# An attention and feed-forward kernel: nine tokens to a partition, head groups on partition halves, x made transposed by wide matmuls

## Chip, cores, metric

One core of one Trainium2 chip. The metric is device time in microseconds (us) of one execution, lower is better; most executions of one kernel agree within 1% (the kernel before: 299.02 to 300.62 in the four beside the changed kernel). Bandwidths are for this one core. "PE" is TensorE's matmul side, DVE VectorE, ACT ScalarE, POOL GpSimd, SP SyncE, which issues nearly all the DMAs.

## The reference, cut to what matters

```python
# q, k, v: (8 batches, 8 heads, 576 tokens, 64) float32
q_s = softmax(q, axis=-1)            # over the 64 of a head
k_s = softmax(k, axis=2)             # over the 576 tokens
kv  = einsum('bhsd,bhse->bhde', k_s, v)
x   = einsum('bhsd,bhde->bhse', q_s, kv)   # -> (8, 576, 512) after the transpose of heads
xn  = (x - mean(x)) / sqrt(var(x) + 1e-6) * g_ln
out = x + relu(xn @ w_ch1) @ w_ch2   # 512 -> 2048 -> 512, all float32
```

## The kernel before: the parts that matter

The feed-forward runs on blocks of 512 tokens (four to a partition, "main"); the last 64 tokens of each batch ("remainder") are collected into a ninth block. `mm1` is the first product (64 matmuls of 512 columns), `mm2_split` the second, done with seven products instead of eight on quarter blocks. A small scheduler in Python orders the instructions; each engine then runs its own list in order (ACT of the changed kernel: a cast of v waits 4.06 us for its load until 110.25, and three relus of matmuls that ended by 108.2 start only after it, from 111.32). Names in the code and the profiles: `stg` are the buffers in which loads land, `ek` and `eq` the exponentials of k and q, `eqT` is `eq` transposed, `vb` is v cast to 16 bits, `kve` (changed kernel) is k'v divided by the softmax sum, `xsT` is x transposed, `ot` the output before its store.

```python
def load_main(b, src):                       # q, k or v: 4 heads at a time, all 128 partitions
    for half in range(2):
        s = nxt("stg", NST)
        load(stg[s].rearrange("p (h r) -> p h r", h=4),
             src[b, 4*half : 4*half + 4, :Q0].rearrange("h (p t) d -> p h (t d)", t=J), ...)  # 1024-byte rows
def load_rem(b, src, row): ...               # the last 64 tokens: 64 partitions, 256-byte rows
# k'v, each head pair g: 4 matmuls over 128 tokens and one over 64
for t in range(KT):
    n = P if t < J else 64
    nc.tensor.matmul(pa[a][:, c0 : c0+130], ek[u][:n, t, g*P : g*P+P],
                     vb[u][:n, t, 2*g : 2*g+2, :], start=(t == 0), stop=(t == KT-1))
# x by tokens: 4 x 4 matmuls of 130 columns (the 65th of each head is the softmax sum), then
# norm(): x = numerator / sum on DVE; then x is DMA-transposed (xsT) for mm1
# ... (cut)
```

The softmax here doesn't subtract the row's maximum and nothing guards it: scores larger than these inputs give would overflow.

## Time and profile before

| | before |
|---|---|
| median of 3 runs | 299.33 us (299.02 to 300.62) |
| PE busy | 283.7 of 299.0 us |
| k'v for one batch, 20 matmuls | 1.87 us |
| undisturbed mm1, mm2 of one block | 13.81 us, 12.25 us |
| 1024-byte load packets, mean / median | 54 / 46 ns |

The last row comes from the trace's records of single DMA packets. A packet of these loads is one row (24,576 packets of 1024 bytes for 48 loads of 512 KB), moved by one of 16 DMA engines; 16 x bytes / time is the rate when all are busy. "Granted clock" (PEclk) is the profile's figure for the share of TensorE's full clock that was granted, 0.997 in the mean here.

Page of the kernel before: the span, PE's busy time, then the span in 40 slices, busy tenths of PE, granted clock, busy tenths of the DMA engines, and GB/s.

```profile
span 299.0 us, 5130 instructions
...
PE 283.7 (95%) x1992; PEld 180.7 (60%) x1992; DVE 200.9 (67%) x482; ACT 151.4 (51%) x271; POOL 22.0 (7%) x40
...
PE   8987999998899999999999999999999999999990
...
PEclk9999999999999999999999999999999999999998
DMA  6999999799799949999999990304303030030006
GB/s 198 288 386 387 367 259 270 220 160 295 239 234 233 321 90 273 343 222 206 304 269 274 244 243 20 140 0 72 140 2 70 3 140 0 2 140 1 2 0 140
```

PE is full; the DMA engines are nearly full too in most of the first 24 slices. The windows of the same kernel cut the span at the first mm1 matmul (24.18), at the first split mm2 (78.59) and at the last matmul. Columns: window, length, then busy time of PE, PEld (weight loads), DVE, ACT and POOL with instruction counts, granted clock, DMA share and GB/s.

```profile
0.00:24.18 24.18, 21.05 (x114) 9.47 (x115) 12.59 (x29) 13.71 (x20) 9.62 (x26) 1.00 0.95 298
24.18:78.59 54.41, 50.37 (x314) 27.34 (x315) 47.13 (x98) 33.62 (x57) 9.09 (x9) 1.00 1.02 281
78.59:291.60 213.01, 212.04 (x1565) 143.86 (x1564) 140.33 (x355) 104.09 (x196) 3.33 (x5) 1.00 0.56 142
291.60:299.00 7.40, 0.27 (x3) 0.00 (x0) 0.88 (x2) 0.00 (x0) 0.00 (x0) 0.87 0.64 142
...
5.00:10.00 5.00, 5.00 (x20) 2.12 (x19) 1.76 (x4) 3.17 (x3) 0.23 (x1) 1.00 1.09 316
```

In the third stretch PE idles 0.97 of 213 us (length minus PE busy), in the second 4.04. The chain of waits (start, length, what) shows one cause of the latter, a late load of v:

```profile
67.12 7.88 DMA stg<-in_v_dram
75.00 0.02 issue
75.02 0.71 DVE vb L343
75.73 0.04 issue
75.77 1.04 PE pa L364 x10
```

### The profile page before, as it was taken

The page shows a single profiled execution, that of the slowest core. Times are in us where ns is not written, and L with a number is a line of the kernel's source. Part 1 is how long each engine was busy: PE and PEld are TensorE (multiplying, and loading weights), DVE is VectorE, ACT ScalarE, POOL GpSimd, SP SyncE. Part 2 cuts the span into 40 slices and gives each one's busy share as a digit, 9 for nine tenths or more (in the row PEclk, how much of TensorE's full clock was granted, in tenths as well). Part 3 has the DMA queues.
Part 4 walks back from the last instruction along what each step waited for, and adds up shares of the span by engine and source line. Part 5 has one row for each costly group of instructions (what it writes and reads, how often), then busy time and mean ns, then how long its engine had stood idle before and what let it go on. Part 6 is the DMA issues. An engine that isn't in the chain of part 4 may idle for free.

```text
span 299.0 us, 5130 instructions
## 1 busy us (share of the span) xinstructions
PE 283.7 (95%) x1992; PEld 180.7 (60%) x1992; DVE 200.9 (67%) x482; ACT 151.4 (51%) x271; POOL 22.0 (7%) x40
## 2 busy tenths in 40 slices
PE   8987999998899999999999999999999999999990
PEld 3444445553696468645875489448747844864780
DVE  0679999995887776677786787657356436635641
ACT  3656476696443990497667740792252055025200
POOL 3432041300000000000000010000000000000000
PEclk9999999999999999999999999999999999999998
DMA  6999999799799949999999990304303030030006
GB/s 198 288 386 387 367 259 270 220 160 295 239 234 233 321 90 273 343 222 206 304 269 274 244 243 20 140 0 72 140 2 70 3 140 0 2 140 1 2 0 140
DMA packets 75127, 53.80 MB, mean 180 GB/s; under 512 B 43872, under 2 KB 68448, under 8 KB 75104
## 3 DMA queue, kind: packets, MB, share of 16 engines
q1 hardware_dynamic: 74528, 53.49, 67.1%
q8 instruction: 15, 0.25, 0.3%
q10 hardware_dynamic: 576, 0.00, 0.1%
q14 instruction: 8, 0.07, 0.1%
HBM read 36.70 MB, written 9.44 MB: 154 GB/s over the span
## 4 chain that ended last, share of the span: by engine, by line
PE 77%; DMA 9%; DVE 7%; ACT 3%; SPq 1%; issue 1%; DVEq 0%
PE pg L516 35%; PE pg L593 30%; DMA stg<-in_v_dram 8%; PE pa L364 4%; PE pg L642 4%; DMA stg<-in_q_dram 2%; PE pa L429 2%; ACT hT L481 1%; PE pg L503 1%; DVE ot L652 1%; SPq L260 1%; DVE bst L723 1%; DVE T L547 1%; DVE vb L343 1%; PE pg L316 1%
## 5 line engine op out<-in xcount | busy, mean ns | idle before, releaser
L516 PE MATMUL pg<-xsT,w_sb 128*128 128x512 f16 x544 | 120.9, 379 | 0.0
L481 ACT ACTIVATE hT<-pg 128x512 f16<-128x512 f32 x122 | 71.4, 595 | 78.9 <-PE pg L516 49.2
L516 PEld LDWEIGHTS <-w_sb 128*128 128x128 f16 x544 | 52.3, 98 | 60.4 <-DVE w_sb L319 0.3
L593 PEld LDWEIGHTS <-S 128*128 128x128 f16 x512 | 49.4, 98 | 5.9
L530 DVE TENSOR_TENSOR S<-hT 128x512 f16<-128x512 f16 x64 | 27.1, 424 | 30.0 <-ACT hT L481 29.0
L593 PE MATMUL pg<-T,S 128*128 128x256 f16 x384 | 44.4, 273 | 0.0
L593 PEld LDWEIGHTS <-hT 128*128 128x128 f16 x384 | 37.2, 98 | 6.7 <-issue 1.2
L593 PE MATMUL pg<-w_sb,hT 128*128 128x256 f16 x256 | 29.6, 272 | 0.3
L601 DVE SCALAR_TENSOR_TENSOR ot<-pg,st,cp 128x256 f32<-128x256 f32 x48 | 21.0, 479 | 12.4 <-PE pg L593 12.3
L601 DVE SCALAR_TENSOR_TENSOR cp<-pg,st,x 128x256 f32<-128x256 f32 x48 | 21.0, 478 | 10.7 <-PE pg L593 10.5
L460 ACT ACTIVATE sq<-x,st 128x512 f16<-128x512 f16 x28 | 20.2, 720 | 5.4 <-DVE st L456 5.0
L390 ACT ACTIVATE eq<-stg 128x1024 bf16<-128x1024 f32 x12 | 12.6, 1058 | 15.8 <-DMA stg<-in_q_dram 15.8
L417 DVE SCALAR_TENSOR_TENSOR x<-pa,rq 128x512 f16<-128x512 f32 x28 | 19.2, 690 | 0.8
L364 PE MATMUL pa<-vb,ek 128*128 128x130 f16 (+1 forms) x160 | 16.5, 223 | 2.9 <-DVE vb L343 2.9
L483 DVE TENSOR_SCALAR hT<-pg 128x512 f16<-128x512 f32 x22 | 15.1, 688 | 6.0 <-PE pg L516 5.6
L337 ACT ACTIVATE ek<-stg 128x1024 bf16<-128x1024 f32 x16 | 16.6, 1052 | 2.6 <-DMA stg<-in_k_dram 2.6
L364 PEld LDWEIGHTS <-ek 128*128 128x128 bf16 (+1 forms) x160 | 11.1, 97 | 9.5 <-issue 3.0
L661 PE MATMUL pg<-zero 128*128 128x512 f16 x54 | 15.5, 443 | 1.2 <-DVE zero L240 1.2
L593 PE MATMUL pg<-w_sb,S 128*128 128x256 f16 x128 | 15.6, 273 | 0.0
L593 PE MATMUL pg<-T,hT 128*128 128x256 f16 x128 | 15.5, 273 | 0.0
L530 DVE TENSOR_TENSOR S<-hT,S 128x512 f16<-128x512 f16 x32 | 14.6, 455 | 0.9
L642 PE MATMUL pg<-w_sb,hT 128*128 128x512 f16 x64 | 15.1, 379 | 0.0
(77 smaller groups left out, 217.9 us busy)
## 6 DMA issues: line engine op xcount, KB each, us to landing
stg<-in_q_dram SPq DMA_DIRECT2D x16, 512.0 KB, 7.4
stg<-in_k_dram SPq DMA_DIRECT2D x16, 512.0 KB, 8.3
stg<-in_v_dram SPq DMA_DIRECT2D x16, 512.0 KB, 6.3
stg<-in_moe_w_ch_dram SPq DMA_DIRECT2D x16, 512.0 KB, 9.4
out_dram<-ot SPq DMA_DIRECT2D x16, 512.0 KB, 2.9
rem<-in_k_dram SPq DMA_DIRECT2D x8, 128.0 KB, 7.7
rem<-in_v_dram SPq DMA_DIRECT2D x8, 128.0 KB, 3.9
rem<-in_q_dram SPq DMA_DIRECT2D x8, 128.0 KB, 5.5
```

The source lines that it names most:

```text
L337: nc.scalar.activation(ek[u][:, :J].rearrange("p t (h d) -> p h t d", h=H)[:, 4 * half : 4 * half + 4], stg[ld["k"][half]].rearrange("p (h ...
L364: nc.tensor.matmul(pa[a][:, c0 : c0 + 130], ek[u][:n, t, g * P : g * P + P], vb[u][:n, t, 2 * g : 2 * g + 2, :], start=(t == 0), stop=(t = ...
L417: plan.add("DVE", 0.76, lambda: nc.vector.scalar_tensor_tensor(dst[:, j, :].rearrange("p (h d) -> p h d", h=H), in0=pz[:, :, :D], scalar=1 ...
L460: plan.add("ACT", act_t(512, 0.15), lambda j=j: nc.scalar.activation(sq, x[:, j, :], AF.Square, bias=sti[:, 1, j : j + 1], accum_out=sti[: ...
L481: nc.scalar.activation(hT[:, m, :], pg[gi], AF.Relu)
L483: nc.vector.tensor_scalar_max(hT[:, m, :], in0=pg[gi], scalar1=0.0)
L516: nc.tensor.matmul(pg[gi], w1_sb[:, ko, m * P : m * P + P], xt[:, ko], start=(ko == 0), stop=(ko == KO1 - 1))
L530: plan.add("DVE", dve_t(512, 2), lambda: nc.vector.tensor_tensor(S[i][:, ks], a, b, op=op), r=r, w=[("S", i, k0), ("S", i, k0 + 1)])
L593: nc.tensor.matmul(pg[gi][:, 256 * i : 256 * i + 256], fa(k, i), fb(k), start=(first and i == 0 and k == 0), stop=(last and k == HK - 1), ...
L601: nc.vector.scalar_tensor_tensor(dst[:, i, :], in0=pg[gi][:, 256 * i : 256 * i + 256], scalar=sti[:, 4, 2 * t0 + i : 2 * t0 + i + 1], in1= ...
L642: nc.tensor.matmul(pg[gis[j]], hT[:, kk, j * P : j * P + P], w2_sb[:, kk, :], start=(kk == 0), stop=(kk == KO2 - 1))
L661: nc.tensor.matmul(bank_, zero[:, :P], zero, start=start, stop=start, skip_group_check=True)
```

## The change

The intent: give each partition nine consecutive tokens (576 = 64 x 9), so that a head fills 64 partitions, the remainder loads vanish, and rows grow to 9 x 64 x 4 = 2304 bytes. Heads 0 to 3 lie on partitions 0 to 63, heads 4 to 7 on 64 to 127. k'v runs on 64 rows of the array, for both halves in turn. The softmax of q is divided out before the product, so x comes out of four 512-column matmuls already transposed, as mm1 wants it, and a DMA transpose brings it back to token order for the norm's statistics and mm2. Relu moves to ACT (138 of its 144 instructions, 122 before), as do the v casts of the later batches. The core of the diff:

```diff
-    def load_main(b, src): ...   def load_rem(b, src, row): ...
+    def load_half(b, src, hf):
+        s = nxt("stg", NST)
+        for e in range(2):
+            load(stg[s][R * e : R * e + R].rearrange("p (h r) -> p h r", h=2),
+                 src[b].rearrange("(e h) (p j) d -> e p h (j d)", e=2, j=JT)[e, :, 2 * hf : 2 * hf + 2],
+                 [("stg", s, e)], 128, 0.295)
 # k'v
-                    for t in range(KT):
-                        n = P if t < J else 64
-                        nc.tensor.matmul(pa[a][:, c0 : c0 + 130], ek[u][:n, t, g * P : g * P + P], ...)
+                for j in range(JT):
+                    for e in range(2):
+                        r0 = R * e
+                        nc.tensor.matmul(pa[ab[e]][:, :130], ek[u][r0 : r0 + R, hf, j, :],
+                                         vb[u][r0 : r0 + R, hf, j].rearrange("p s d -> p (s d)"),
+                                         start=(j == 0), stop=(j == JT - 1))
 # x, transposed (kve: k'v divided by the sum, off-diagonal blocks masked to zero)
+        for g in (0, 2, 1, 3):
+            nc.tensor.matmul(pa[a], kve[u][:, g, :], et[:, g % 2, 0:8, c0 : c0 + R], start=True, stop=True)
+    def tokens(c, cls=1):
+        nc.sync.dma_start_transpose(x..., xsT...)        # then bn_stats, bn_aggr on DVE
 # stores: one of 128 partitions -> two of 64
+        for e in range(2):
+            nc.sync.dma_start(out[c].rearrange("(p j) c -> p j c", j=JT)[:, 4*hf + e : 4*hf + e + 3 : 2, :], ot[o][R*e : R*e + R])
 # ... (norm, remainder block, square sums cut)
```

## The prediction

> **What bounds the kernel now.** TensorE. The page gives PE 283.7 of 299.0 us busy, PEclk full. By windows: 0 to 24.2 us is loading and attention of batch 0; from the first mm1 matmul (24.18) to the last matmul (291.6) PE idles only about 5 us; the end takes 7.4. In the middle mm1 costs 13.81 a batch and the split mm2 12.25 (chain of waits, from 201 on); the change leaves these alone. It can touch the 24.2, about 23 us of attention matmuls (groups L364, L429 and smaller), the 5 us and the tail. DMA is saturated until 80 us (share 0.95 to 1.05); its late v load costs 2.1 us at 73.7 (chain: stg<-in_v_dram, L343, L364).
>
> **Removed, added, moved.**
> - DMA: 1024-byte rows (54 ns a packet) and 256-byte remainder rows (12,288 packets) become 2304-byte rows; 2048-byte weight rows took 88 ns, so 370 GB/s against about 320. Transposes grow from 28.7k to 32.3k rows of about 22 ns. Estimate: 25 us less DMA time, mostly off the path.
> - PE, k'v: 20 matmuls, 1.87 us a batch, become 36 on 64 rows. In the raw order of L364 a switch between 128 and 64 rows costs 100 ns (starts 152 to 160 ns apart against 55): 8 a batch, then 4. [...] the trace shows it for column halves only: L439's pairs start 14 ns apart, each 61 ns. Estimate 18 x 30 + 200 = 0.74 us a group, 1.5 a batch; without overlap 2.4.
> - PE, x: 16 matmuls of 130 columns (0.94) plus 0.37 per two batches become 4 of 512 (0.86) and 4 of 64 (0.22). Even.
> - DVE: norm (0.69+0.20+0.08, x28) and relu go; reduce (1.34 each), bn_stats (0.665), kve come. Roughly even.
> - ACT: squares go (20 us); all relu (0.595), v casts (1.2), xT copies come: about 170 us, still under PE.
> - x reaches mm1 without a DMA transpose; the transposed x is for mm2 only.
> - Last stores: 2 DMAs a half instead of 4, 0.6 us of SP issue each.
>
> **On the path.** Start: v lands again about 15.5, but kve, copies and weight centring follow faster on DVE: mm1 at about 21.4 (-2.8). DVE still limits centring (PE waits 3 us before the fifth m) and batch 1's attention, so mm1 of batch 1 starts near 59, like now. The v stall and its neighbours in 70 to 80 go: -3.5. Attention on PE: -3 over batches 1 to 7. Tail: -1.3. New stalls of in-order ACT (v cast waiting for DMA ahead of relu) and kve on DVE: +1.
>
> Sum: 299.3 - 3.5 - 3 - 1.3 + 1 = about 292. Range 287.5 to 297.5. Faster by over 2% (under 293.3): 0.58; within 2%: 0.38; slower: 0.04.
>
> **What would show it.** k'v matmuls in pairs 10 to 15 ns apart, 0.7 to 0.8 us a group of 18; first mm1 at 20.5 to 22.5; no PE gap over 1 us from 60 to 90; mm1 13.81 and mm2 12.25 unchanged; last matmul to end about 6 us; DMA share below 0.8 after 90.
>
> **What would make it wrong.** Row halves not overlapping (+6); SP blocked behind an x transpose waiting for xsT, so inputs come late (+1 to 4); ACT at 75% in mm1 holding pg banks; POOL's multiply (2.3 us, from 1.04 for 512 columns) delaying the eqT transpose and the v load gated on it.

## The result, and the profile after

312.27 us (median of 4 runs, 311.5 to 314.11) against 299.5 (4 runs): the ratio is 1.043, 95% interval 1.037 to 1.0489. It got slower. A ratio here is the mean time of one kernel's fast runs over the mean of the other's fast runs of the same rounds, so it is not quite the ratio of the medians quoted. All runs discussed are fast; slow ones, among them one run of the kernel before at 1032 us, are left out of the ratios. The changed kernel's mean granted clock was 0.984: two stretches of 3.4 us, from 23.3 and from 112.0, had a granted clock of 0.50, and both came just after gaps of PE (1.73 and 3.32 us); after the gap of 1.73 before 60.04 there was none (1.00 from 60 to 90). At half the clock they cost at most 3.4 us together (an estimate, half of twice 3.4 us). I take them for a consequence of the waiting below and not a cause of its own; no run here shows it.

The same lines of the page, after:

```profile
span 309.6 us, 5175 instructions
...
PE 280.9 (91%) x2017; PEld 173.5 (56%) x2017; DVE 197.4 (64%) x407; ACT 161.8 (52%) x258; POOL 36.6 (12%) x32
...
PE   8749798779999959999898979999999999999992
...
PEclk9997999999999979999999999999999999999998
DMA  7999999999996999269989990999993440013004
GB/s 160 267 273 386 280 332 238 236 255 214 228 226 108 196 259 217 54 159 228 233 160 234 286 181 4 210 215 224 160 269 82 83 115 22 2 23 115 0 1 138
```

PE has less to do than before (280.9 against 283.7), yet the span is 10.6 us longer: waiting, not work. The windows, cut at the same events (first mm1 27.07, first split mm2 82.60, last matmul 303.40), and two stretches in which only q, k and v load:

```profile
0.00:27.07 27.07, 19.94 (x117) 8.67 (x118) 13.43 (x27) 11.27 (x16) 3.73 (x15) 0.94 0.96 255
27.07:82.60 55.53, 47.85 (x293) 24.83 (x292) 49.62 (x86) 33.25 (x54) 11.39 (x7) 1.00 1.07 265
82.60:303.40 220.80, 212.98 (x1609) 140.03 (x1607) 133.49 (x294) 117.29 (x189) 21.44 (x10) 0.99 0.66 145
303.40:309.60 6.20, 0.09 (x1) 0.00 (x0) 0.88 (x2) 0.00 (x0) 0.00 (x0) 0.76 0.60 169
...
5.00:10.00 5.00, 4.00 (x16) 1.52 (x14) 2.42 (x3) 2.08 (x2) 0.23 (x1) 1.00 1.06 225
...
45.00:65.00 20.00, 16.17 (x116) 7.90 (x114) 17.46 (x32) 8.00 (x11) 3.42 (x3) 1.00 1.05 235
```

Read the last two lines first: the DMA engines are fully busy (1.05), and move 225 to 235 GB/s. Before, 1024-byte rows moved at 316 in the same first stretch. The rows are longer, the rate is lower. (Had half of the 16 engines stood idle, the share would be about 0.5; so all of them work, and slowly. From 45 to 65 the kernel before moved only 220 GB/s, but with 256-byte rows, transposes and stores among its packets; the first stretch is the clean comparison.) PE's timeline (start, length, line, operation; in brackets the idle time before it and who ended it) shows what that does:

```profile
20.55 0.70 PE L379 MATMUL pa<-vb,ek 64*128 64x130 f16 x18 [2.33 <-DVE vb L369]
22.97 0.94 PE L379 MATMUL pa<-vb,ek 64*128 64x130 f16 x18 [1.73 <-DVE vb L369]
...
27.07 3.22 PE L473 MATMUL pg<-xsT,w_sb 128*128 128x256 f16 x28
...
60.04 0.70 PE L379 MATMUL pa<-vb,ek 64*128 64x130 f16 x18 [1.73 <-DVE vb L369]
...
85.32 0.70 PE L379 MATMUL pa<-vb,ek 64*128 64x130 f16 x18
...
111.47 0.72 PE L379 MATMUL pa<-vb,ek 64*128 64x130 f16 x18 [3.32 <-ACT vb L372]
```

k'v itself is as cheap as hoped: the raw starts show a pair every 59 ns, its two matmuls 3 to 4 ns apart in ten of the 16 groups and 18 to 19 in six (medians of a group), and 0.63 us from a group's start to the next instruction (0.70 with the modelled end). But it waits for v: the DVE casts of v began at 19.7 and 22.2 us, where before they began at 15.4. DVE's timeline of the changed kernel shows that they had waited for the loads:

```profile
19.73 0.77 DVE L369 CAST vb<-stg 128x1152 f16<-128x1152 f32 x1 [2.17 <-DMA stg<-in_v_dram]
22.16 0.76 DVE L369 CAST vb<-stg 128x1152 f16<-128x1152 f32 x1 [1.67 <-DMA stg<-in_v_dram]
```

The packet records say it most directly:

| kernel | load packet | mean, median ns | 16 x bytes / mean |
|---|---|---|---|
| before | 1024 B | 54.0, 46 | 304 GB/s |
| changed | 2304 B | 159.9, 166 | 231 GB/s |
| before and changed: weights, in stretches of weights alone | 2048 B | 88 | 372 GB/s |

In proportion to the 88 ns of a 2048-byte weight row, a 2304-byte row would take 99 ns (an estimate). It took 160. What differs from weight rows: the load covers 64 partitions and not 128 (theory A: a load into one half of the partitions is slow); the row is 2304 bytes long (rival B); there are twice as many loads, 0.6 to 0.7 us of SP issue each (2.63 us for four loads of k at 4.87; rival C).

### The profile page after: what moved, and what is told of

Same layout as the page of the kernel before. It is cut to its first block, busy times and chain, and to the rows that moved or that the text cites. A ratio compares the mean times of both kernels' runs of the same rounds, so it can differ in the third digit from the quotient of the medians.

```text
span 309.6 us, 5175 instructions
## 1 busy us (share of the span) xinstructions
PE 280.9 (91%) x2017; PEld 173.5 (56%) x2017; DVE 197.4 (64%) x407; ACT 161.8 (52%) x258; POOL 36.6 (12%) x32
## 5 line engine op out<-in xcount | busy, mean ns | idle before, releaser
L450 ACT ACTIVATE hT<-pg 128x512 f16<-128x512 f32 x138 | 80.7, 598 | 61.5 <-PE pg L486 55.3
L486 PE MATMUL pg<-xsT,w_sb 128*128 128x512 f16 x480 | 109.3, 382 | 2.3 <-DVE ot L570 1.2
L502 DVE TENSOR_TENSOR S<-hT 128x1024 f16<-128x1024 f16 x32 | 23.8, 748 | 55.6 <-ACT hT L450 55.6
L332 POOL TENSOR_TENSOR eq<-eq,rzq 128x1152 bf16<-128x1152 bf16 x12 | 25.8, 2155 | 145.8 <-issue 52.3
L324 ACT ACTIVATE eq<-stg 128x1152 bf16<-128x1152 f32 x16 | 18.6, 1169 | 21.3 <-DMA stg<-in_q_dram 21.3
L439 DVE BATCH_NORM_STATS2 bst<-x 128x6 f32<-128x512 f16 x36 | 24.0, 668 | 5.4 <-DMA x<-xsT 5.4
L327 DVE TENSOR_REDUCE zq<-eq 128x18 f32<-128x1152 bf16 x16 | 21.4, 1340 | 7.3 <-ACT eq L324 7.3
L364 ACT ACTIVATE ek<-stg 128x1152 bf16<-128x1152 f32 x16 | 18.7, 1167 | 13.8 <-DMA stg<-in_k_dram 13.7
L379 PE MATMUL pa<-vb,ek 64*128 64x130 f16 x288 | 11.4, 220 | 10.6 <-DVE vb L369 6.6
L372 ACT CAST vb<-stg 128x1152 f16<-128x1152 f32 x12 | 14.0, 1168 | 8.1 <-DMA stg<-in_v_dram 8.0
```

The costliest lines, as they stand in the source:

```text
L324: plan.add("ACT", act_t(QW), lambda hf=hf, e=e: nc.scalar.activation(e.rearrange("p j (s d) -> p s j d", s=2), sv(lq[hf]), AF.Exp), r=sk(l ...
L327: plan.add("DVE", dve_t(QW), lambda hf=hf, eh=eh: nc.vector.reduce_sum(zq[:, hf], eh, axis=AX.X), r=[("eq", u, hf)], w=[("zq", hf)], cls=cls)
L332: plan.add(eng, dve_t(QW) if early else 2.6, lambda hf=hf, eh=eh, e2=e2: e2.tensor_tensor(eh, eh, rzq[:, hf].to_broadcast([P, 2 * JT, D]), ...
L364: plan.add("ACT", act_t(QW), lambda hf=hf: nc.scalar.activation(ek[u][:, hf].rearrange("p j (s d) -> p s j d", s=2), sv(lk[hf]), AF.Exp), ...
L379: nc.tensor.matmul(pa[ab[e]][:, :130], ek[u][r0 : r0 + R, hf, j, :], vb[u][r0 : r0 + R, hf, j].rearrange("p s d -> p (s d)"), start=(j == ...
L439: plan.add("DVE", dve_t(512), lambda j=j: nc.vector.bn_stats(bst[:, j, :], x[:, j, :]), r=[(xk, j)], w=[("bst", j)], cls=cls)
```

## The experiments

Each q/k/v experiment (e1 to e5, e7, e10) keeps the order of the compute instructions of PE, DVE, ACT and (but in e5, where POOL itself issues loads) POOL exactly as in the kernel it starts from, so that only the DMAs differ.

### e1: one load of 128 partitions

```diff
-        for e in range(2):
-            load(stg[s][64*e : 64*e+64]..., 64 partitions, 2 rows of 2304 bytes)
+        rows = src[b].rearrange("h (p j) d -> (h p) (j d)", j=JT).rearrange("(h p) r -> p h r", p=P)
+        load(stg[s].rearrange("p (h r) -> p h r", h=2), rows[:, 2*hf : 2*hf + 2], ...)
```

> The changed kernel, every engine's order kept, but each pair of 64-partition loads is one load of 128 partitions with the same 2304-byte rows (heads land at other partitions, so the result is wrong on purpose). Theory A [...]: the 2304-byte packets fall from a median of 166 ns to about 96 to 104, the first mm1 comes at 21 to 23 us instead of 27.1, and the time falls to 291 to 297 us. Theory B (rows of 2304 bytes are slow in themselves): packets stay near 165 ns and the time near 312. Theory C (twice as many DMAs, 0.6 us of issue each): packets stay as they are but the waits between them go, and the time falls.

Measured: 296.95 us against 300.87 (ratio 0.988, interval 0.9803 to 0.9957; three rounds). Its output is wrong, which doesn't matter for the time. The packets: mean 104.8, median 93 ns, 352 GB/s. The windows of e1, cut at its own first mm1, first split mm2 and last matmul:

```profile
0.00:21.79 21.79, 18.25 (x118) 8.18 (x119) 13.06 (x26) 11.22 (x16) 4.08 (x15) 1.00 0.89 326
21.79:72.78 50.99, 47.60 (x294) 24.73 (x293) 49.00 (x87) 32.72 (x55) 11.07 (x7) 1.00 0.95 280
72.78:287.20 214.42, 210.46 (x1607) 139.33 (x1607) 133.41 (x294) 115.56 (x189) 21.43 (x10) 1.00 0.55 151
287.20:293.60 6.40, 0.29 (x3) 0.01 (x1) 0.88 (x2) 0.00 (x0) 0.00 (x0) 0.89 0.57 164
...
5.00:10.00 5.00, 3.74 (x19) 1.58 (x18) 3.24 (x4) 3.06 (x3) 0.59 (x1) 1.00 1.02 379
```

The same bytes in the same rows now move at 379 GB/s in the first stretch of loads, mm1 starts at 21.79 instead of 27.07, and the profiled span falls by 16.0 us. Against the kernel before this is a gain of only 1.2%. B falls: 2304-byte rows are fast. A and C remain.

### e3: two loads again, each over all partitions

```diff
-            load(stg[s][64*e : 64*e+64]..., both rows)
+            load(stg[s]..[:, e : e+1], rows[:, 2*hf + e : 2*hf + e + 1], ...)   # 128 partitions, one row each
```

> Like e1, but two loads again, each over all 128 partitions with one row of 2304 bytes per partition: the number of DMAs is that of the changed kernel (result wrong on purpose). Theory A: as e1, packets 96 to 104 ns and within 2 us of it. Theory C: near the changed kernel, 308 us or more. Theory B: near the changed kernel too, packets near 165 ns.

Measured (one round): 296.4 us, ratio 0.9866 (0.9772 to 0.996), packets mean 103.9, median 93 ns, the profiled span equal to e1's (293.6). The number of loads is that of the changed kernel, so C falls.

### e4: the same partitions, cut elsewhere

```diff
+            cuts = (slice(32, 96),) if e == 0 else (slice(0, 32), slice(96, 128))
```

> Like e1 again (same data), but cut as partitions 32 to 95 in one load and 0 to 31 and 96 to 127 in two more. [...] half of the packets take about 100 ns and half about 165, two clear groups, and the time lies between e1 and the changed kernel. If every load of 64 or fewer partitions is slow [...], all packets stay near 165 ns.

This asks what "half" means: whether any load of 64 partitions is slow, or only the load of an end half. Measured: 310.03 us (ratio 1.032, 1.0192 to 1.0448; two executions); the interval reaches the changed kernel's 1.043, so the time decides nothing. The packets say more: their mean is 140 ns, and those in the fastest 10 ns bin (90 to 100 ns) are 36% of all; 10% in the changed kernel, 80% in e1. Sorted by start time and folded by tile (256 packets), the eighths of the cycle have medians of 144, 113, 95, 95, 101, 148, 155 and 144 ns; in e1 all eight are 93. The load of 32 to 95 is issued first, and 46% of the first half of the cycle but 27% of the second lie in the fastest bin. So 64 partitions in the middle can be filled as fast as 128 (95 ns against 93), and 64 at an end are not (166 ns in the changed kernel). This rules out that any load of 64 partitions is slow, and leaves A for the halves at an end; why the middle differs from them no run here shows. It is not as clean as expected: half of the packets should have been fast, and since the trace doesn't name a packet's load, which packets are the fast ones is read from their order alone.

### e2: the suspected cost put into the kernel before

```diff
+            for e in range(2):
+                cut = slice(64*e, 64*e + 64)
+                nc.sync.dma_start(dst[cut], src[cut])      # main loads of q, k, v only
```

> The kernel before, order kept, result right, but each main load of q, k and v is cut into two loads of 64 partitions; rows stay 1024 bytes. Theory A: the 1024-byte packets go from a median of 46 ns to 70 to 80, and the time from 299.5 to 305 to 312 us, like the changed kernel. Theory B: nothing happens, 299 to 301. Theory C: packets stay at 46 to 54 ns and the time rises with the number of issues, by 1 to 5 us.

### e7: its control, cut by heads instead of partitions

```diff
-                cut = slice(64*e, 64*e + 64);  dst[cut], src[cut]
+                cut = slice(2*e, 2*e + 2);     dst[:, cut], src[:, cut]
```

> Control for e2: the kernel before, each main load also cut into two, but by heads: each covers all 128 partitions (result right). Same number of loads as e2. Theory A: 1024-byte packets at 46 to 54 ns and 299 to 304 us. If e2's 328 us came from the number of loads that SP issues (theory C), this one is slow too, above 315 us.

Measured: e2 327.91 us (ratio 1.0911, 1.0831 to 1.0991), packets mean and median 79 ns instead of 54 and 46; e7 301.19 us (ratio 1.0043, 0.9968 to 1.0117), packets 54.5 and 46. Both results right. The same stretch of q/k loads, in the windows of e2 and then of e7:

```profile
5.00:10.00 5.00, 4.33 (x20) 1.81 (x18) 0.49 (x1) 2.11 (x2) 0.23 (x1) 1.00 1.15 214
```

```profile
5.00:10.00 5.00, 5.00 (x20) 2.09 (x19) 1.81 (x4) 3.17 (x3) 0.23 (x1) 1.00 1.03 303
```

214 GB/s by partition halves, 303 by heads, with the same number of loads and the same row length. A's packet time was right (70 to 80 expected); its total was not: I expected 305 to 312 us and got 328. The 24,576 packets grew by 25 ns each, 39 us over 16 engines, and the kernel before has little slack for it: its DMA engines were already nearly full in most of the first 24 of 40 slices.

### e5 and e10: both halves in flight from two queues

```diff
-            load(stg[s][64*e : ...], ...)                         # both from SP
+            load(stg[s][64*e : ...], ..., nc.gpsimd if e else nc.sync)   # e5
+            load(stg[s][64*e : ...], ..., nc.scalar if e else nc.sync)   # e10
```

> The changed kernel with the same 64-partition loads, but the upper half of each pair is issued from the POOL queue instead of SP, so both halves can be in flight together (result right). [...] 2304-byte packets fall from 166 ns median to 95 to 125, and the time to 294 to 303 us. If a load of 64 partitions is slow whatever runs beside it, packets stay above 150 ns and the time near 312.

> What e5 left open: the changed kernel with the upper-half loads issued from ACT (same kind of queue as SP, rows stay 2304 bytes), so that both halves are in flight together. Theory A: packets fall from 166 ns median to 95 to 125 where both queues run, whatever the time does; ACT's order is burdened with the issues and their buffer waits, so the time may be anywhere from 296 to 315 us. If the limit is 64 partitions per load, packets stay above 150 ns.

Both missed. e5: 365.13 us (ratio 1.2175), SP's packets still at a mean of 173 ns; POOL's loads became 4608-byte packets of 372 ns, so it is not a clean comparison. e10's packets are comparable: 357.14 us (ratio 1.1911), packets mean 167, median 174 ns on both queues, though both ran at once (from 6 to 8 us 94 packets started from SP's queue and 111 from ACT's). The total tells nothing, since ACT now waits for buffers and issue before its exponentials, which did not start until after 15 us. The packet times do: two half loads side by side (174 ns) don't make a whole one (93 in e1). That two halves in flight together would reach a whole load's packet time was my guess, and no trace had shown it. In e10 the cost stayed with each half load, although a load of the other half ran beside it. Why the two streams don't interleave to better effect no run here shows.

### e6: a mend with the right result

e1's load is one uniform stretch of memory because partition half e then holds head 4hf+2s+e. k'v and x can follow that if each head gets its own 64 x 64 tile of the array, and no mask is needed:

```diff
+        load(stg[s]..., rows[:, 2*hf : 2*hf + 2], ...)             # 128 partitions
-                    for e in range(2):
-                        nc.tensor.matmul(pa[ab[e]][:, :130], ek[u][r0 : r0+R, hf, j, :], ...)
+                    for i in range(2):
+                        for e in range(2):
+                            r0, s0 = R * e, R * i
+                            nc.tensor.matmul(pa[ab[e]][s0 : s0+R, :VW], ek[u][r0 : r0+R, hf, j, s0 : s0+R],
+                                             vb[u][r0 : r0+R, hf, j, i], ...)
+                for e in range(2):                                  # x: head (hf, i, e)
+                    for i in range(2):
+                        nc.tensor.matmul(pa[xbk[2*hf + i]][R*e : R*e+R], kve[u][R*i : R*i+R, 2*e + hf, :],
+                                         et[R*i : R*i+R, hf, 0:8, R*e : R*e+R], ...)
```

> A mend with the right result: heads are dealt so that partition half e holds head 4hf+2s+e, then 128 partitions are one uniform stretch of rows and one load fills them; k'v and x use 64x64 tiles (72 small matmuls for k'v instead of 36, 8 and 8 for x, no mask). Theory A: packets at 93 ns as in e1 and time within 3 us of e1's 296.4, ratio to before 0.975 to 0.995, if four small tiles run side by side (0.6 to 1.0 us for the 36 matmuls of one half). If small tiles don't run side by side, 36 take about 2 us, and the time is 299 to 306.

### e8: and v no longer behind the eqT transpose

```diff
-            gate[0] = state["eqT"]        # v loads waited in SP's order for the transpose of eq
```

> e6 with one line less: v loads no longer wait in SP's order for the eqT transpose of the same batch. In e1 the v cast on ACT waited 4.4 us for its load and PE idled with it 1.6 us once. If those waits are what is left, this is 1 to 3 us faster than e6; if the transpose then comes late behind v, it is the same or slower.

Measured on the same chip, three rounds each: e6 289.62 us (ratio 0.9655, 0.961 to 0.9699), e8 288.26 (ratio 0.9616, 0.9567 to 0.9665), both right. A repeat of e8 with five rounds:

> e8 once more with five rounds beside e9 on the same chip, for the interval: 287.5 to 289.5 us, ratio 0.957 to 0.967.

288.12 us against 299.62 (ratio 0.961, 0.9572 to 0.9648). e8 beats both kernels. Page, windows and timeline of its first run:

```profile
span 285.9 us, 5798 instructions
...
PE 274.1 (96%) x2376; PEld 168.8 (59%) x2376; DVE 188.9 (66%) x407; ACT 160.7 (56%) x266; POOL 35.9 (13%) x29
```

```profile
0.00:21.75 21.75, 19.62 (x168) 8.63 (x168) 13.45 (x28) 11.37 (x17) 3.93 (x12) 1.00 0.89 325
21.75:73.64 51.89, 49.06 (x426) 25.35 (x425) 48.60 (x93) 37.15 (x62) 10.76 (x7) 1.00 1.04 315
73.64:279.80 206.16, 205.44 (x1784) 134.85 (x1783) 126.29 (x287) 112.15 (x190) 21.18 (x10) 1.00 0.54 147
279.80:285.90 6.10, 0.00 (x0) 0.00 (x0) 0.59 (x2) 0.00 (x0) 0.00 (x0) 0.75 0.61 173
```

```profile
79.84 0.48 PE L373 MATMUL pa<-vb,ek 64*64 64x65 f16 x36
...
98.21 0.63 PE L392 MATMUL pa<-eqT,kve 64*64 64x512 bf16 x8
```

In the third stretch PE idles 0.72 us; in e1 it was 3.96 and in the changed kernel 7.82. The 36 small matmuls of a group take 0.41 us to the next instruction, where 18 larger took 0.63, and x's eight take 0.56 where four took about 0.86 (4 x 0.216). By the raw starts four small matmuls follow the four before them after about 33 ns at 65 columns and 240 ns at 512. That is cheaper than I expected of e6 (0.6 to 1.0 us a group), and e6 came out 3.8 us below its expected range (293.4 to 299.4): 16 groups of k'v at 0.22 us less and 8 of x at 0.30 less make 5.9 of the 7.3 us between e1 and e6, an estimate. e8 over e6 is 1.4 us in the medians: the v cast waited 1.5 us for loads instead of 2.7, and PE idled 0.7 instead of 1.6 us from 78.59 to 279.80. The scheduler moved other instructions in e6 and e8 too, so these gains are not split further.

### e9: stores from two queues

```diff
-                nc.sync.dma_start(out..., ot[o][R*e : R*e+R])
+                (nc.scalar if e else nc.sync).dma_start(...)
```

> e8 with the upper-half stores issued from ACT instead of SP. The traces so far show most 64-partition stores at 84 ns per 2048-byte packet, as fast as whole ones, so I expect no change of the packets; the two last stores no longer queue behind each other on SP (0.6 us of issue each), worth 0 to 1 us at the end, against some 0.6 us issues inside ACT. Time within 0.5% of e8. [...]

Measured in five rounds: 289.42 us (ratio 0.9657, 0.9622 to 0.9693) against e8's 288.12, so 0.45% slower: within the 0.5%, but the gain at the end did not come. Stores that read half the partitions are not slow throughout: in e8's last 10 us, when nothing else moves, their 2048-byte packets have a median of 84 ns and a mean of 115, with 194 of 512 over 120; whole stores before took a mean of 173 ns for 4096 bytes, 86 for 2048. But the kernel before also stores its last block from 64 partitions at a time, and its 512 packets of 2048 bytes in the last 10 us have a median of 156 and a mean of 147. The loads of halves, which write to these partitions, took 160 for 2304. So half stores are slow at times, and what decides it no run here shows. The second queue does not change the packets: the mean of all 2048-byte ones is 104.9 ns in e8 and 104.3 here.

## Why the prediction was wrong, point by point

**The step that failed** is the first entry under "Removed, added, moved": "1024-byte rows (54 ns a packet) and 256-byte remainder rows (12,288 packets) become 2304-byte rows; 2048-byte weight rows took 88 ns, so 370 GB/s against about 320". It priced a load by its row length alone. A row of 2304 bytes took 160 ns in the changed kernel, 231 GB/s, because each load covers one half of the partitions; with all partitions (e1) it took 105. Instead of the "25 us less DMA time" of the same entry there were 33 us more: SP's queue (its lines in the pages of the kernel before, the changed kernel and e1: packets, MB, share of 16 engines) took 200.7 us of 16 engines before, 233.9 in the changed kernel and 187.4 in e1, so that even with whole loads the gain is 13 and not 25.

```profile
q1 hardware_dynamic: 74528, 53.49, 67.1%
q1 hardware_dynamic: 56096, 54.41, 75.6%
q1 hardware_dynamic: 55328, 54.40, 63.8%
```

With it fell "v lands again about 15.5": the cast of v's first half began at 19.7.

How much it cost: e1 differs from the changed kernel in the loads only, and its profiled span is 16.0 us shorter (309.6 to 293.6). The miss was 312.3 - 292 = 20 us. In spans, 299.0 and the forecast -6.8 make 292.2, and e1 has 293.6.

The other terms can be held against e1, where the loads are what I had assumed:

- Start: mm1 at 21.4 forecast, 21.79 in e1 (27.07 in the changed kernel). Right.
- "The v stall and its neighbours ... go: -3.5". The first split mm2 starts at 72.78 in e1. Before it was 78.59, of which 1.87 was k'v of batch 2, which e1 does later; so 76.7 to 72.8, -3.9. Right. In the changed kernel it is 82.60, +5.9.
- "Attention on PE: -3". In the third stretch PE is busy for 210.46 us in e1 and 212.04 before, and e1's has batch 2's k'v in it (2 x 0.63). So -2.8. Right.
- k'v on row halves: 0.74 us a group forecast, 0.63 measured, pairs 3 to 4 or 18 to 19 ns apart, not 10 to 15. That row halves run side by side was assumed in the forecast and not shown by the trace before; the changed kernel shows it, with two matmuls every 59 ns. Right, a little better.
- mm1 13.81 and mm2 12.25 a block unchanged: 13.81 and 12.23 in the changed kernel's chain. Right.
- End: "about 6 us": 6.2. Right.
- New stalls "+1": PE's idle time in the third stretch went from 0.97 to 3.96 us in e1, so +3; undersized by 2. One of them, 1.63 us at 99.6 in e1, is the v cast waiting for its load, one of the two risks that I named; with e6's tiles and without the gate (e8) the idle time is 0.72.
- "No PE gap over 1 us from 60 to 90" and "DMA share below 0.8 after 90" were to show the plan right. Neither sign caught the miss. From 60 to 90 the largest gap of the changed kernel is 0.90 us (the 1.73 ends at 60.04, just outside), and its DMA share after 90 is 0.65 (0.54 before). What showed it was the first mm1 at 27.07 and the gap of 3.32 us before 111.47.

"Row halves not overlapping (+6)" was the risk that I put first. The halves that cost the time were those of the loads (160 ns a packet against 105 in e1), not of the array.

## What to carry to other kernels

A layout that puts work on partition halves is still best loaded in transfers that cover all partitions (here a 2304-byte packet took a mean of 105 ns so, and 160 in loads of halves); choose which rows go to which half so that 128 partitions are one uniform stretch, and let the compute side (here 64 x 64 tiles) adapt. When DMA engines are fully busy at a rate below what another load in the same trace reaches (here 231 GB/s, and 372 for the weights), compare packet times by partitions covered as well as by row length. A converse test, the suspected cost put into the good kernel beside a control with the same count of transfers, settles such a question in two runs.
